# Chunked state scan feeding a gated feed-forward: the scan of chunks 2 to 5 rearranged by pairs, with B and C turned on VectorE

## The chip, the cores and the metric

One core of a Trainium2 chip runs the whole program, in one launch. The metric is the device time of one execution in microseconds: 369.13 us for the kernel before, the median of three runs (368.94 to 369.47). TensorE (PE) has two clock levels, 1.2 and 2.4 GHz; the profile gives the granted clock as a share of the higher one.

## The reference

```python
# x (4, 8, 768, 32), a (4, 8, 768), B and C (4, 8, 768, 16): batch, head, position, width
state = np.zeros((batch, H, N, D))
for c in range(S // 32):                      # 32 positions at a time
    xc, Bc, Cc, la = ...                      # la = log(clip(a, 1e-6, 1))
    cum = np.cumsum(la, axis=-1)
    M = einsum('bhin,bhjn->bhij', Cc, Bc) * tril(exp(cum_i - cum_j))
    y_intra = einsum('bhij,bhjd->bhid', M, xc)
    y_inter = einsum('bhin,bhnd->bhid', Cc, state) * exp(cum)
    y[:, :, sl] = y_intra + y_inter
    state = exp(sum(la)) * state + sum_j(Bc x xc * exp(cum_last - cum_j))
x = y as rows of 8 * 32 = 256, 3072 of them
out = (sigmoid(x @ w_gate) * (x @ w_val)) @ w_out      # 256 -> 1536 -> 256
```

How long the pieces are in which the state is carried on doesn't change the result; the kernel takes 64 positions.

## The kernel before

**Tiling.** The sequence is cut into 6 chunks (`c`) of 128 positions. A chunk of one batch entry `b` is a unit, `u = 4 c + b`; two units make a pair. The scan of a unit gives 128 rows of `x`, its two halves of 64 positions being the pieces between which a state is carried. The feed-forward pass of chunk `k` takes 512 rows at once: 12 groups `f` of 128 hidden columns, each with a gate and a value product (`pg`, `pv`, six matmuls each since operands are split into a high and a low part), then four output projections (`po`). Chunk 0 has cheaper passes with fewer parts.

**The scan of a unit** (class `Unit`, `results`). `products` (L424): TensorE turns B and C by two transposes against the identity (L431, L432) into a PSUM tile `pt`, ScalarE copies them out (L435) and writes two copies of C masked by `of_g` (L437), so that a strip of 32 partitions, which holds two heads, gives the products of each head apart. `multiply` (L486): 16 matmuls C B of a pair into `pcb` (L495). `decays`: a scan on VectorE makes the decays `ab` (L450), GpSimd multiplies B by the last of them (`bd`, L460) and C by the running products `pp` (`cd`, L472). `weigh`: VectorE multiplies the products by the decays (`m`, L509). `results`, for a pair: sums within the halves (`inside`, L526), what each half adds to the state (`keep`, L537), VectorE masks that (`chosen`, L545) and carries the state on (L572, L482), then the products of C and the state accumulate into the same PSUM columns (L581). ScalarE and VectorE take the sum out as a high and a low part of `x` (L595, L601).

**What sets the order.** Every step yields its engine, an estimated cost, what it needs and what it makes. A planner in `run` (L193) keeps a clock for each engine from these estimates and always takes the step that could start first; among those within 0.1 us the one with the earliest due time, from the call or the table `DUES` (L18). Each engine then runs its instructions in that fixed order. The scan of chunk `c` is due during the pass of chunk `c - 1`, so its pieces on TensorE stand between gate, value and projection groups. SP issues all loads and stores of that time in one queue. Three PSUM buffers serve gate, value and projection groups. The decays go through DRAM (`a_z`, `a_p`) to be spread over partitions.

Of the kernel before, what the change touches and what calls it, by code (L numbers as in the profile page):

```python
# [50 lines left out]
P0 = 18.0  # L51
# [6 lines left out]
UNIT_T = 14.9  # L58
UNIT_D = 0.0
# [12 lines left out]
def tile_ssd_then_gated_ffn(  # L72
# [26 lines left out]
    NPRE = 5  # L99
# [190 lines left out]
    def pair_of(tag, c, b, shape):  # L290

        k = tag, c, b // 2
        if k not in got:
            got[k] = ld.tile([P, 2, H, shape], F32, tag=tag, name=f"{tag}{c}_{b // 2}", bufs=2)
        return got[k]

    def load_bc(c, b, n):
        cs = slice(c * L, (c + 1) * L)
        for tag, src in (("bn", b4), ("cn", c4)):
            t = pair_of(tag, c, b, N)  # L300
            nc.sync.dma_start(
                t[:, b % 2 : b % 2 + n].rearrange("p b h n -> p (b h) n"), src[cs, b * H : (b + n) * H]
            )

# [22 lines left out]
    def load_p(c, b):  # L327
        t = ld.tile([P, L], F32, tag="pp", name=f"pp{c}_{b}", bufs=NPRE)
        src = a_p[b, :, c * L : (c + 1) * L].rearrange("h (o l) -> h o l", o=1).broadcast_to([H, N, L])
        nc.sync.dma_start(t, src)  # L330
        got["pp", c * NB + b] = t
# [80 lines left out]
    def state_of(u, name):  # L412

        return wk.tile([P, NG * D], F32, tag=f"st{u % NB}", name=f"{name}{u}", bufs=3)

    class Unit:


        def __init__(self, c, b):
            self.c, self.b, self.u = c, b, c * NB + b  # L420
            self.nm = f"{c}_{b}"
            self.more = c < NCH - 1

        def products(self):  # L424
# [9 lines left out]
            self.bct = wk.tile([P, 4, L], F32, tag="bct", name=f"bct{self.nm}", bufs=4)  # L434
# [21 lines left out]
        def decayed(self):  # L456
            c, b, u = self.c, self.b, self.u
            eng = yield step(("dve", "pool"), (0.28, 0.42), [("bc" if c else "b0", u if c else u // 2), ("scan", u), ("y", u - 4)], [("bdec", u)], port=True)
# [6 lines left out]
        def before(self):  # L465
# [5 lines left out]
            self.cd = wk.tile([P, L], F32, tag="cd", name=f"cd{self.nm}", bufs=4)  # L471
            engines[eng].tensor_tensor(out=self.cd, in0=self.bct[:, 1], in1=got["pp", u], op=ALU.mult)  # L472

        def last(self, i):
            return got["pp", self.u][:, i * L2 + L2 - 1 : (i + 1) * L2]

        def state(self):
# [3 lines left out]
            states[u] = state_of(u, "sn")  # L481
            nc.vector.scalar_tensor_tensor(  # L482
                out=states[u], in0=self.s1, scalar=self.last(1), in1=self.after, op0=ALU.mult, op1=ALU.add
            )

# [64 lines left out]
    def results(*two):  # L550
# [3 lines left out]
        c, more = two[0].c, two[0].more  # L554
# [4 lines left out]
        yield step("pe", 0.2 + 0.45 * n, needs, [("y", u) for u in us], port=96 * n if more else 80 * n)  # L559
        py = two[0].banks[:, :, 2 * L :].rearrange("p (i k) (s u l) -> p i k s u l", i=2, s=2, l=L2)  # L560
        for k, t in enumerate(two):
            within(
                t, lambda i, kt, rows: py[rows, i, kt, 0, k], lambda i, rows: py[rows, i, 0, 1, k], lambda kt: k == 0, more
# [5 lines left out]
        for k, (t, u) in enumerate(zip(two, us)):  # L569
            yield step("dve", 0.24, [("S", u - NB), ("pp", u), ("inter", u - NB)], [("first", u)], port=True)  # L570
            t.s1 = state_of(u, "sm")
# [3 lines left out]
        yield step("pe", 0.2 + 0.3 * n, [("cd", u) for u in us], [("inter", u) for u in us], port=32 * n)  # L575
# [11 lines left out]
        for i in range(2):  # L587
# [8 lines left out]
            end = {"cb": -1} if i and not more else {}  # L596
            made = [("x", c, t.b) for t in two] if i else []
            if i and not more:
                made += [(k, u) for u in us for k in ("lo", "S", "after")]
            yield step("dve", DVE_HALF, [], made, **end)  # L600
            nc.vector.tensor_tensor(out=lo, in0=y, in1=hi.bitcast(F32), op=ALU.subtract)  # L601
        if more:
            yield step("dve", 0.25, [("S", u - 2) for u in us], [(k, u) for u in us for k in ("lo", "after")], cb=-1)
            ml = wk.tile([P, n, NG * D], F32, tag="mr", name=f"mr{two[0].nm}")
            chosen(ml, py[:, 1, 0, 1], n)
            for k, t in enumerate(two):
                t.after = ml[:, k]

    class FirstUnit(Unit):
# [21 lines left out]
        def before(self):  # L631
# [3 lines left out]
            self.cd = wk.tile([P, L], F32, tag="cd", name=f"cd{self.nm}", bufs=4)  # L635
# [78 lines left out]
    def first_states(late):  # L714
# [9 lines left out]
        if late:  # L724
            for b in range(NB):
                i, k = b // 2, b % 2
                yield step("dve", 0.24, [("p0",)], [("S", b)] + ([("first", 2), ("first", 3)] if b == NB - 1 else []), port=True)
                states[b] = state_of(b, "sn")
# [107 lines left out]
    def value(k, f):  # L836
# [124 lines left out]
    a_p = dr.tile([NB, H, S], F32, name="a_p")  # L961
    a0 = const.tile([2 * NB * H, L], F32, name="a0")
# [4 lines left out]
    az, ap = (hp.tile([NB * H, S], F32, tag=f"h{10 - i}", name=f"a{i}") for i in range(2))  # L967
# [44 lines left out]

    def loads_of(c, b, n):
# [4 lines left out]
            "b": load(2, 1.6 * n, [(k, u) for k in ("tp", "bdec") for u in old], [("bc", u) for u in us], lambda: load_bc(c, b, n)),  # L1018
# [3 lines left out]
    def decays_of(c, b):  # L1022
        u = c * NB + b
        return {
            "a": load(2, 0.95, [("mult", u - NDEC), ("bdec", u - NDEC), ("a_z",)], [("a", u)], lambda: load_a(c, b)),
            "p": load(1, 0.3, [("cd", u - NPRE), ("S", u - NPRE), ("a_p",)], [("pp", u)], lambda: load_p(c, b)),
        }

    def initial():
# [3 lines left out]
        made += [("S", u) for u in range((NCH - 1) * NB, NCH * NB)]  # L1033
# [12 lines left out]
        "p": load(1, 2.3, [("p",)], [("a_p",)], save_p),  # L1046
    }
# [20 lines left out]
    def unit(due, c, b):  # L1068
        u = Unit(c, b) if c else FirstUnit(c, b)
        if c > 0:  # L1070
            if b % 2 == 0:
                for k, g in loads_of(c, b, 2).items():
                    task(due - AHEAD, f"{k}{u.nm}", g)
            for k, g in decays_of(c, b).items():
                task(due - AHEAD, f"{k}{u.nm}", g)
        else:
            task(-9.0 + b, f"spread{b}", u.spread())
        if c or b > 1:
            task(due, f"before{u.nm}", u.before())
        if c:  # L1080
            task(due, f"products{u.nm}", u.products())
        task(due, f"decays{u.nm}", u.decays())
        if c == 0 and b % 2:
# [7 lines left out]
        elif b % 2:  # L1091
            if u.u < NB * NCH - 1:
# [4 lines left out]
        if u.more and c:  # L1097
            task(due + STATE, f"state{u.nm}", u.state())

# [4 lines left out]
    for b in range(NB):  # L1104
        unit(UNIT1 + UNIT1_D * b, 1, b)
    for i in range(NW):
# [3 lines left out]
    for k in range(NCH):  # L1110
        for b in range(NB):
# [49 lines left out]
```

## Time and profile before

| | |
|---|---|
| median of 3 runs | 369.13 us |
| profiled execution | 369.12 us |
| its span | 367.3 us |
| TensorE busy | 359.9 us, 98% |
| VectorE, ScalarE, GpSimd busy | 157.1, 150.4, 152.5 us |
| granted TensorE clock | 1.00 |

The span is from the first to the last instruction of the profiled execution. fp32 matmuls leave two records each in the trace. Matmuls are pipelined: the duration of one overlaps the next, so what a piece costs is read from when the following one starts, and the chain of waits lists exactly these steps.

### The profile page before, as it was taken

What the parts mean: (1) busy time and instruction counts of PE and PEld (TensorE: products, weight loads), DVE (VectorE), ACT (ScalarE), POOL (GpSimd) and SP (SyncE); (2) the same over time, 40 slices, a digit from 0 to 9 for tenths busy, and PEclk for the clock granted to TensorE, in tenths of its full rate; (3) what the DMA queues carried; (4) which work ended last, traced back from release to release, by engine and by line L of the source; (5) the groups of instructions that cost most, each with busy time, mean ns of one, the idle gap of its engine ahead of it and who ended that gap; (6) DMA issues with size and microseconds to landing.
All of it is one profiled execution on the core that took longest, in us unless ns stands there. A gap on an engine that the chain in (4) does not pass through costs nothing.

```text
span 367.3 us, 8116 instructions
## 1 busy us (share of the span) xinstructions
PE 359.9 (98%) x3372; PEld 285.8 (78%) x3372; DVE 157.1 (43%) x279; ACT 150.4 (41%) x309; POOL 152.5 (42%) x160
## 2 busy tenths in 40 slices
PE   8999899999999999999999999999999999999996
PEld 3567478778878788788788877788877888888885
DVE  5779478774326650253551225432243510223201
ACT  2575875324573411544411454421445420343400
POOL 5435865645896400445410355520244330154410
PEclk9999999999999999999999999999999999999999
DMA  7999975545033431314031015321000000000000
GB/s 164 220 246 214 322 222 150 87 62 142 0 30 87 63 85 55 33 57 59 16 87 53 21 12 107 43 32 37 31 2 2 2 0 29 30 0 0 2 29 29
DMA packets 89270, 26.27 MB, mean 72 GB/s; under 512 B 76306, under 2 KB 82002, under 8 KB 89234
## 3 DMA queue, kind: packets, MB, share of 16 engines
q1 hardware_dynamic: 85074, 25.37, 30.1%
q10 hardware_dynamic: 4160, 0.39, 0.9%
q8 instruction: 26, 0.43, 0.5%
q14 instruction: 10, 0.08, 0.1%
HBM read 22.41 MB, written 3.34 MB: 70 GB/s over the span
## 4 chain that ended last, share of the span: by engine, by line
PE 92%; DVE 1%; ACT 1%; issue 0%
PE pv L893 25%; PE pg L893 25%; PE po L931 15%; PE po L932 7%; PE po L920 6%; PE pcb L526 2%; PE pcb L581 2%; PE pcb L495 2%; PE pv L790 1%; PE pg L790 1%; PE pcb L537 1%; PE pv L884 1%; PE pg L884 1%; PE pt L431 1%; PE po L928 1%; PE pt L432 1%
## 5 line engine op out<-in xcount | busy, mean ns | idle before, releaser
L861 POOL TENSOR_TENSOR h<-g,h 128x512 fp32r<-128x512 f32 x60 | 78.9, 1315 | 153.8 <-ACT h L859 153.3
L893 PE MATMUL pv<-xh,w 128*128 128x512 f32 x264 | 94.0, 397 | 0.0
L893 PE MATMUL pg<-xh,w 128*128 128x512 f32 x264 | 93.7, 395 | 0.0
L855 DVE TENSOR_TENSOR g<-pv,g 128x512 f32<-128x512 f32 x60 | 41.5, 692 | 97.4 <-PE pv L893 94.4
L931 PE MATMUL po<-w,h 128*128 128x512 f32 x228 | 81.9, 402 | 0.0
L859 ACT CAST h<-g 128x512 fp32r<-128x512 f32 x60 | 37.2, 621 | 79.7 <-DVE g L855 79.7
L932 PE MATMUL po<-w,h 128*128 128x256 f32 x228 | 64.0, 281 | 0.0
L893 PEld LDWEIGHTS pg<-xh,w 128*128 128x128 f32 x264 | 49.5, 188 | 11.1 <-issue 0.4
L893 PEld LDWEIGHTS pv<-xh,w 128*128 128x128 f32 x264 | 49.6, 188 | 10.7 <-issue 0.5
L893 PE MATMUL pg<-xl,w 128*128 128x512 f32 x132 | 51.5, 390 | 0.0
L893 PE MATMUL pv<-xl,w 128*128 128x512 f32 x132 | 51.5, 390 | 0.0
L931 PEld LDWEIGHTS po<-w,h 128*128 128x128 f32 x228 | 42.8, 188 | 11.0 <-issue 0.3
L834 ACT ACTIVATE g<-pg 128x512 f32<-128x512 f32 x68 | 40.8, 600 | 13.9 <-PE pg L893 13.5
L932 PEld LDWEIGHTS po<-w,h 128*128 128x128 f32 x228 | 43.1, 189 | 0.2
L949 DVE TENSOR_TENSOR o<-po,o 128x256 f32<-128x256 f32 x20 | 8.5, 425 | 53.7 <-ACT o L947 53.7
L947 ACT COPY o<-po 128x256 f32<-128x256 f32 x20 | 7.5, 373 | 54.7 <-PE po L932 54.1
L394 POOL TENSOR_TENSOR w<-wr,w 128x512 fp32r<-128x512 f32 x18 | 25.3, 1406 | 9.1 <-ACT w L392 9.1
L893 PEld LDWEIGHTS pg<-xl,w 128*128 128x128 f32 x132 | 24.8, 188 | 5.1 <-issue 0.2
L893 PEld LDWEIGHTS pv<-xl,w 128*128 128x128 f32 x132 | 24.8, 188 | 4.5
L377 POOL TENSOR_TENSOR wr<-wr 128x512 int32<-128x512 int32 x18 | 20.4, 1140 | 13.5 <-ACT wr L375 7.4
L450 DVE TENSOR_TENSOR_SCAN ab<-ab,delta 128x512 f32<-128x512 f32 x20 | 24.9, 1256 | 0.8 <-DMA ab<-a_z 0.8
L920 PE MATMUL po<-wr,h 128*128 128x256 f32 x96 | 23.4, 393 | 0.0
(105 smaller groups left out, 368.2 us busy)
## 6 DMA issues: line engine op xcount, KB each, us to landing
ab<-a_z SPq DMA_DIRECT2D x40, 128.0 KB
wr<-in_moe_w_gate_dram SPq DMA_DIRECT2D x6, 512.0 KB
wr<-in_moe_w_val_dram SPq DMA_DIRECT2D x6, 512.0 KB
wr<-in_moe_w_out_dram SPq DMA_DIRECT2D x6, 512.0 KB
out_dram<-o SPq DMA_DIRECT2D x24, 128.0 KB
xn<-in_x_dram SPq DMA_DIRECT2D x10, 256.0 KB
bn<-in_B_dram SPq DMA_DIRECT2D x10, 128.0 KB
cn<-in_C_dram SPq DMA_DIRECT2D x10, 128.0 KB
```

What stands on the lines that cost most here:

```text
L377: nc.gpsimd.tensor_tensor(out=lw.bitcast(I32), in0=hw.bitcast(I32), in1=lw.bitcast(I32), op=ALU.add)
L394: engines[eng].tensor_tensor(out=lo, in0=lw, in1=hi.bitcast(F32), op=ALU.subtract)
L450: nc.vector.tensor_tensor_scan(out=t.rearrange("p h l -> p (h l)"), data0=t.rearrange("p h l -> p (h l)"), data1=delta.rearrange("p h l -> ...
L834: nc.scalar.activation(gs[k, f], pm, AF.Sigmoid)
L855: nc.vector.tensor_tensor(out=g, in0=pm, in1=g, op=ALU.mult)
L859: copies[eng](hh, g)
L861: engines[eng].tensor_tensor(out=hl, in0=g, in1=hh.bitcast(F32), op=ALU.subtract)
L893: nc.tensor.matmul(pm, w[:, part, kt, fs], xx[:, kt], start=(i == 0), stop=(i == 3 * NK - 1))
L920: nc.tensor.matmul(acc[:, :DM], hs[k, f][:, js], whole[NF + f // 2][:, f % 2], start=start, stop=stop, skip_group_check=True,)
L931: nc.tensor.matmul(acc, hh, w.rearrange("p i m -> p (i m)"), start=start, stop=False, skip_group_check=True)
L932: nc.tensor.matmul(acc[:, :DM], hl, w[:, 0, :], start=False, stop=stop, skip_group_check=True)
L949: nc.vector.tensor_tensor(out=o, in0=acc[:, DM:], in1=o, op=ALU.add)
```

## The change

From chunk 2 on, pairs replace units (class `Pair`; chunks 0 and 1 stay as they are).

- B and C are loaded as rows of 64 numbers by eight DMAs into `tn`, 32 partitions of positions for each strip, and one VectorE instruction turns its 32 x 32 blocks (`turn`). In the result a strip of 32 partitions holds two heads of one unit, where before each strip held two heads `2q`, `2q + 1` of the unit in hand; the two units of the pair lie side by side. B is loaded as before as well (`bn`); C no more.
- The decay products are written to DRAM a second time in that order (`a_q`, four DMAs), and the states of chunk 1 are copied into it by 16 small copies of 32 partitions (`shuffled`).
- On TensorE, `block` issues without a break the products across of one pair (`across`), the products C B of the pair after next (`meet`) and the sums within of the pair between (`one_inside`, `kept`). The blocks follow one another in a chain of needs.
- Products across get PSUM columns of their own; ScalarE copies the sums within out (`inner`), VectorE adds the products across (`result`), and the low part of `x` may be taken by GpSimd.
- `az` and `ap` change their tiles, so that the value product of group 9 of chunk 0 waits for `a_z` and that of group 10 for `a_q`.

```diff
 DUES = {
-    "r": -31, "w6": -30, "w9": -25, "w11": 13, "w12": 14, "w13": 15, "w14": 16, "w15": 12.7, "w16": -2.4, "w17":
...
+    "decays3_0": 144.7, "inner5_2": 189.4, "decays5_1": 159.1, "b4_2": -39.7, "inner4_0": 101.9, "decays4_2": 139.1,
...
+    def load_t(c, b):
+        t = ld.tile([P, 2, 2 * NG, RUN * N], F32, tag="tn", name=f"tn{c}_{b // 2}", bufs=1)
+        got["tn", c, b // 2] = t
+        for q in range(NQ):
+            for k, src in enumerate((Bm, Cm)):
+                rows = src.rearrange("b h s n -> (b h) (s n)")[b * H + 4 * q : b * H + 4 * q + 4]
+                nc.sync.dma_start(
+                    t[32 * q : 32 * q + 32, k],
+                    rows[:, c * L * N : (c + 1) * L * N].rearrange("h (s x) -> s h x", x=RUN * N),
+                )
...
+    def shuffled(late):
+        for k in range(2):
+            for m in range(NQ):
+                u, q, j = NB + 2 * late + k, 2 * k + m // 2, m % 2
+                last = [("pS", 2 + late)] if k and m == NQ - 1 else []
+                eng = yield step(("act", "pool"), (0.22, 0.2), [("S", u)], last)
...
+    def meet(pcb, t):
+        t.banks = pcb
+        for j in range(2):
+            for q in range(NQ):
+                qs = slice(32 * q, 32 * q + 32)
+                for i in range(2):
+                    half = slice(i * L2, (i + 1) * L2)
+                    nc.tensor.matmul(
+                        pcb[half, q, j * L : (j + 1) * L], t.bt(j)[qs, half], t.cm(j)[qs, :, half], start=True, stop=True
+                    )
...
+    def kept(t, i, out, start=True):
+        for j in range(2):
+            for m in range(2):
+                at = 32 * (t.b % 2 * 2 + m)
+                keep_one(t, i, 2 * m + j, out[at : at + 32, j * NG * D : (j + 1) * NG * D], start and j == 0)
+
+    def across(out, state, cd):
+        for j in range(2):
+            for i in range(2):
+                for q in range(NQ):
+                    qs = slice(32 * q, 32 * q + 32)
+                    nc.tensor.matmul(
+                        out[q][j * L2 : (j + 1) * L2, i * L2 : (i + 1) * L2], state[i][qs, j],
+                        cd[qs, j, i * L2 : (i + 1) * L2], start=True, stop=True, skip_group_check=True,
+                    )
+
+    class Pair:
...
+        def turn(self):
+            p = self.p
+            yield step("dve", 1.15, [("tn", p)] + ..., [("turn", p)], port=True)
+            self.bct = wk.tile([P, 8, L], F32, tag="bct", name=f"bct{self.nm}", bufs=2)
+            nc.vector.transpose(
+                self.bct[:, :4].rearrange("p k (b r) -> p r k b", r=RUN),
+                got["tn", self.c, self.p % 2].rearrange("p k h (r n) -> p r (k h) n", n=N),
+            )
+            yield step("act", 1.02, [], [("masked", p)])
+            for g in range(NG):
+                nc.scalar.mul(
+                    self.bct[:, 4:].rearrange("p (j g) l -> p j g l", g=NG)[:, :, g], self.bct[:, 2:4], of_g[:, g : g + 1]
+                )
...
+        def inner(self):
...
+            nc.scalar.copy(self.y.rearrange("p i k u l -> p (i k) (u l)"), fixed["banks"][:, :, 2 * L : 3 * L])
+
+        def result(self):
...
+                if k:
+                    for m in range(2):
+                        nc.vector.tensor_tensor(out=y[:, m], in0=outer[m], in1=y[:, m], op=ALU.add)
+                else:
+                    more = fixed["banks"][:, :2, 3 * L :].rearrange("p m (i l) -> p m i l", i=2)
+                    nc.vector.tensor_tensor(out=y, in0=more, in1=y, op=ALU.add)
...
+                nc.scalar.copy(hi, y)
+                eng = yield step(("dve", "pool"), (DVE_HALF, 0.76), [], ..., port=True)
+                engines[eng].tensor_tensor(out=lo, in0=y, in1=hi.bitcast(F32), op=ALU.subtract)
+
+    def block(n, last, cb, now):
+        needs, makes, cost, instructions, buffers = [("block", n - 1)], [("block", n)], 0.3, 0, {}
+        if last:
+            needs += [("pfirst", last), ("pcd", last), ("added", last - 1)]
...
+        if cb:
+            needs += [("masked", cb)] + ([("mult", t.u) for t in pairs[cb - 1].two] if cb > FIRST_P else [])
...
+        if now:
+            needs += [(k, t.u) for t in pairs[now].two for k in ("mult", "bdec")]
+            needs += [("xnp", now), ("inner", now - 1), ("pafter" if now < 2 * NCH - 1 else "pfirst", now - 1)]
...
-                7: [("scan", 3)], 8: [("p",)], 9: [("a_p",)], 10: [("a_z",)],
+                7: [("scan", 3)], 8: [("p",)], 9: [("a_z",)], 10: [("a_q",)],
...
+    blocks = [(None, 4, None), (None, 5, 4)] + [(p - 1, p + 1, p) for p in range(5, 2 * NCH - 1)]
+    blocks += [(2 * NCH - 2, None, 2 * NCH - 1), (2 * NCH - 1, None, None)]
```

TensorE in the pass of chunk 1, before: the first pair of chunk 2 (`pcb_1360`), its products and its sums; `pt` is a transpose of B or C of another unit, `pg` and `pv` are gate and value groups.

```order
L893 MATMUL pg_7_1345<-xh_965,w_599 128x512
L495 MATMUL pcb_1360<-bct_0_1156 64x128 x8
L495 MATMUL pcb_1360<-bct_1_1341 64x128 x8
L431 MATMUL pt_2_1379<-eye,bn_1_1028 128x128
L432 MATMUL pt_2_1379<-eye,cn_1_1030 128x128
L893 MATMUL pv_7_1385<-xh_965,w_617 128x512
...
L893 MATMUL pv_8_1419<-xh_965,w_677 128x512
L526 MATMUL pcb_1360<-m_0_1392,xn_0_929 32x64 x16
L537 MATMUL pcb_1360<-xn_0_929,bd_0_1101 32x64 x8
L526 MATMUL pcb_1360<-m_1_1398,xn_0_929 32x64 x16
L537 MATMUL pcb_1360<-xn_0_929,bd_1_1201 32x64 x8
L893 MATMUL pg_9_1481<-xh_965,w_637 128x512
```

TensorE in the same pass, now: block 2, with the products across of chunk 2's first pair (`cd2_0`), the products of chunk 3's first (`bct3_0`) and the sums of chunk 2's second (`m2_2`, `m2_3`).

```order
L1147 MATMUL pv1_4_1432<-xh1_941,w5_1204 128x512
L715 MATMUL banks_1172<-cd2_0_1263,sq0_1018 64x64 x3
L715 MATMUL local_1268<-cd2_0_1263,sq0_1018 64x64
L715 MATMUL banks_1172<-cd2_0_1263,sm4_1355 64x64 x3
L715 MATMUL local_1268<-cd2_0_1263,sm4_1355 64x64
...
L673 MATMUL banks_1172<-bct3_0_1386 64x128 x16
L689 MATMUL banks_1172<-m2_2_1349,xn2_1_1169 32x64 x16
L689 MATMUL banks_1172<-m2_3_1359,xn2_1_1169 32x64 x16
L696 MATMUL local_1268<-xn2_1_1169,bd2_2_1165 32x64 x4
L696 MATMUL banks_1172<-xn2_1_1169,bd2_2_1165 32x64 x4
...
L1147 MATMUL pg1_5_1533<-xh1_941,w4_1149 128x512
```

Pieces that stood alone between full-size groups now stand in one run, of three different pairs, and no transpose of B or C is among them.

VectorE in the pass of chunk 1, before: value products (`g1_5` and so on) around the weighting of chunk 2's first pair (`m2_0`, `m2_1`).

```order
L855 TENSOR_TENSOR g1_5_1308<-pv1_5_1301,g1_5_1308 128x512
L855 TENSOR_TENSOR g1_6_1334<-pv1_6_1327,g1_6_1334 128x512
L509 TENSOR_TENSOR m2_0_1392<-pcb8_1360,ab2_0_810 128x512
L509 TENSOR_TENSOR m2_1_1398<-pcb8_1360,ab2_1_748 128x512
L855 TENSOR_TENSOR g1_7_1377<-pv1_7_1385,g1_7_1377 128x512
L855 TENSOR_TENSOR g1_8_1426<-pv1_8_1419,g1_8_1426 128x512
L450 SCALAR_TENSOR_TENSOR ab3_2_1400<-ab3_2_1400,delta_100 128x512
```

VectorE at the start of the same pass, now: between block 0 and block 2.

```order
L682 TENSOR_TENSOR m2_0_1206<-banks_1172,ab2_0_800 128x512
L682 TENSOR_TENSOR m2_1_1213<-banks_1172,ab2_1_897 128x512
L740 STREAM_TRANSPOSE bct2_2_1230<-tn2_1_1109 128x4x128
L1109 TENSOR_TENSOR g1_0_1225<-pv1_0_1217,g1_0_1225 128x512
L1109 TENSOR_TENSOR g1_1_1265<-pv1_1_1254,g1_1_1265 128x512
L682 TENSOR_TENSOR m2_2_1349<-banks_1172,ab2_2_946 128x512
L582 TENSOR_TENSOR ml2_0_1353<-local_1268,mask_102 128x128
L682 TENSOR_TENSOR m2_3_1359<-banks_1172,ab2_3_1020 128x512
L659 SCALAR_TENSOR_TENSOR sm4_1355<-sq0_1018,pp2_0_1190,ml2_0_1353 128x64
L740 STREAM_TRANSPOSE bct3_0_1386<-tn3_0_1243 128x4x128
L1109 TENSOR_TENSOR g1_2_1368<-pv1_2_1361,g1_2_1368 128x512
```

The weightings of chunk 2 have moved to the start of the pass, and two of the eight new transposes stand among them and the first value products.

## Rows read from the trace of the kernel before

**Rows 1.** Page, busy time of each engine and granted clock in 40 slices.

```profile
PE 359.9 (98%) x3372; PEld 285.8 (78%) x3372; DVE 157.1 (43%) x279; ACT 150.4 (41%) x309; POOL 152.5 (42%) x160
...
PEclk9999999999999999999999999999999999999999
```

**Rows 2.** Waits of TensorE, longest in total: us in total, times, longest us.

```profile
PE pt L431 <- ACT bct L437: 1.0, 1, 1.0
...
PE pcb L526 <- DVE m L509: 0.2, 1, 0.2
```

**Rows 3.** Table by stage: from:to, length, PE, PEld, DVE, ACT, POOL busy, clock, DMA.

```profile
88.57:144.88 56.31, 56.31 (x568) 46.10 (x567) 24.46 (x41) 23.63 (x48) 30.21 (x29) 1.00 0.26 53
144.88:201.49 56.61, 56.61 (x569) 46.23 (x569) 21.75 (x40) 20.67 (x44) 18.94 (x20) 1.00 0.27 52
201.49:258.43 56.94, 56.94 (x571) 46.43 (x571) 19.36 (x38) 21.68 (x47) 19.96 (x21) 1.00 0.23 42
258.43:314.50 56.07, 56.07 (x536) 45.62 (x535) 16.73 (x30) 19.92 (x41) 16.80 (x15) 1.00 0.04 11
314.50:367.30 52.80, 49.54 (x241) 41.52 (x239) 10.85 (x18) 16.50 (x29) 15.48 (x12) 1.00 0.05 15
```

**Rows 4.** Chain that ended last, in order of time: start us, us, what.

```profile
80.09 3.82 PE po L920 x16
...
114.37 0.38 PE pcb L526 x32
114.75 0.20 PE pcb L537 x9
...
115.28 0.21 PE pcb L537 x12
115.49 1.59 PE pg L893 x6
...
265.26 0.11 PE pt L431
...
266.87 1.36 PE pg L893 x6
268.23 0.62 PE pcb L495 x32
268.85 1.59 PE pv L893 x6
...
288.54 0.62 PE pcb L581 x32
```

**Rows 5.** TensorE in order of time, chunk 0: start us, us, instruction, records.

```profile
20.42 0.86 PE L526 MATMUL pcb<-m,xn 64*32 64x64 f32 x64
21.20 0.69 PE L691 MATMUL pcb<-cd,m 32*64 32x64 f32 x32
```

**Rows 6.** Groups on VectorE by form: count, busy us, mean ns, idle before.

```profile
L450 DVE TENSOR_TENSOR_SCAN ab<-ab,delta 128x512 f32<-128x512 f32 x20 | 24.9, 1256 | 0.8 <-DMA ab<-a_z 0.8
L509 DVE TENSOR_TENSOR m<-pcb,ab 128x512 f32<-128x512 f32 x24 | 15.7, 686 | 5.8 <-PE pcb L495 5.6
...
L572 DVE SCALAR_TENSOR_TENSOR sm<-sn,pp,ml 128x64 f32<-128x64 f32 x20 | 7.9, 426 | 0.4
...
L545 DVE TENSOR_TENSOR ml<-pcb,mask 128x128 f32<-128x128 f32 x10 | 2.9, 290 | 15.9 <-PE pcb L537 15.9
...
L996 DVE TENSOR_TENSOR_SCAN a<-a,a 32x768 f32<-32x768 f32 x1 | 2.9, 2864 | 0.0
```

**Rows 7.** Group on ScalarE, masked copies of chunk 0.

```profile
L659 ACT ACTIVATE bct<-pt,of_g 128x256 f32<-128x256 f32 x4 | 1.7, 479 | 0.0
```

**Rows 8.** SP in order of time: start us, us, DMA issues.

```profile
49.24 5.54 SPq L322 DMA_DIRECT2D ab<-a_z  x8
...
57.40 1.13 SPq L322 DMA_DIRECT2D ab<-a_z  x2
```

**Rows 9.** VectorE in order of time, scans of chunk 1: start us, us, idle before.

```profile
61.32 1.23 DVE L450 TENSOR_TENSOR_SCAN ab<-ab,delta 128x512 f32<-128x512 f32 x1 [0.82 <-DMA ab<-a_z]
...
67.69 2.06 DVE L450 TENSOR_TENSOR_SCAN ab<-ab,delta 128x512 f32<-128x512 f32 x1
```

More of the change, by code (lines that the diff above doesn't have):

```diff
@@ L57 @@
 FFN1 = 82.0
-UNIT_T = 14.9
-UNIT_D = 0.0
+EARLY = (15.0, 35.0)
 AHEAD = 46.7
@@ L292, in pair_of @@
         k = tag, c, b // 2
+        if tag == "cn" and k not in got:
+            both = ld.tile([P, 2, 2, H, N], F32, tag="tn", name=f"cn{c}", bufs=1)
+            for late in range(2):
+                got[tag, c, late] = both[:, late]
         if k not in got:
@@ L484, in state, with cd_of @@
             )
+    def cd_of(u):
+        k = "cd", u // 2
+        if k not in got:
+            got[k] = wk.tile([P, 2, L], F32, tag="cd", name=f"cd{u // 2}", bufs=2)
+        return got[k][:, u % 2]
     def multiply(pcb, at, *us):
@@ L553, in results @@
         n = len(two)
-        c, more = two[0].c, two[0].more
+        c = two[0].c
         for t, u in zip(two, us):
@@ L595, in results @@
             nc.scalar.copy(hi, y)
-            end = {"cb": -1} if i and not more else {}
             made = [("x", c, t.b) for t in two] if i else []
-            if i and not more:
-                made += [(k, u) for u in us for k in ("lo", "S", "after")]
-            yield step("dve", DVE_HALF, [], made, **end)
+            yield step("dve", DVE_HALF, [], made)
             nc.vector.tensor_tensor(out=lo, in0=y, in1=hi.bitcast(F32), op=ALU.subtract)
[L602 to L607, printed above, removed]
+        yield step("dve", 0.25, [("S", u - 2) for u in us], [(k, u) for u in us for k in ("lo", "after")], cb=-1)
@@ new lines, in results @@
+        ml = wk.tile([P, n, NG * D], F32, tag="mr", name=f"mr{two[0].nm}")
+        chosen(ml, py[:, 1, 0, 1], n)
+        for k, t in enumerate(two):
+            t.after = ml[:, k]
+    def shuffled(late):
[4 more added lines that the diff above has]
+                eng = yield step(("act", "pool"), (0.22, 0.2), [("S", u)], last)
+                if 2 + late not in states2:
+                    states2[2 + late] = state_of(late, "sq")
+                (nc.scalar.copy if eng == "act" else nc.gpsimd.tensor_copy)(
+                    states2[2 + late][32 * q : 32 * q + 32, j], states[u][32 * m : 32 * m + 32]
+                )
@@ new lines, in spread_out, with one_inside @@
+    def spread_out(t, pcb):
+        k = t.b % 2
+        t.m = wk.tile([P, H, L2], F32, tag="m", name=f"m{t.nm}", bufs=4)
+        by = "p (q h) l -> p q (h l)"
+        nc.vector.tensor_tensor(
+            out=t.m.rearrange(by, q=2), in0=pcb[:, 2 * k : 2 * k + 2, : 2 * L], in1=t.dec.rearrange(by, q=2), op=ALU.mult
+        )
+    def one_inside(t, i, kt, r, out, start):
+        half, h = slice(i * L2, (i + 1) * L2), NQ * kt + r
+        nc.tensor.matmul(
+            out, got["xn", t.c, t.b // 2][half, t.b % 2, h], t.m[half, h], start=start, stop=True, skip_group_check=True
+        )
@@ L966, in tile_ssd_then_gated_ffn @@
     )
-    az, ap = (hp.tile([NB * H, S], F32, tag=f"h{10 - i}", name=f"a{i}") for i in range(2))
+    az, ap = (hp.tile([NB * H, S], F32, tag=f"h{9 + i}", name=f"a{i}") for i in range(2))
     load_first("cn", c4, 0, N, nc.scalar)
@@ L1032, in initial @@
         made = [(k, u) for k in keys for u in range(-6, 0)]
-        made += [("S", u) for u in range((NCH - 1) * NB, NCH * NB)]
+        made += [(k, p) for k in ("plo", "pafter", "inner", "added") for p in range(2, FIRST_P)] + [("block", -1)]
         made += [("used", i) for i in (-2, -1)] + [(k, u) for k in ("cd", "inter") for u in range(2)]
@@ L1096, in unit @@
             pair.append(u)
-        if u.more and c:
+        if c:
             task(due + STATE, f"state{u.nm}", u.state())
+            if b % 2:
+                task(due + STATE, f"shuffle{b // 2}", shuffled(b // 2))
     task(-20.0, "products0", first_products())
@@ L1105, in tile_ssd_then_gated_ffn @@
         unit(UNIT1 + UNIT1_D * b, 1, b)
+    starts = [P0, FFN1] + [FFN1 + (2 * NF * GV_T / 2 + NB * PROJ_T) * k for k in range(1, NCH)]
+    for c in range(2, NCH):
+        for b in range(NB):
+            unit(starts[c - 2] + EARLY[b // 2] if c > 2 or b > 1 else starts[1] - EARLY[0], c, b)
+    blocks = [(None, 4, None), (None, 5, 4)] + [(p - 1, p + 1, p) for p in range(5, 2 * NCH - 1)]
+    blocks += [(2 * NCH - 2, None, 2 * NCH - 1), (2 * NCH - 1, None, None)]
+    for i, (last, cb, now) in enumerate(blocks):
+        if i < 4:
+            due = starts[1] + (2.0, 10.0, 25.0, 40.0)[i]
+        else:
+            due = starts[2 + (i - 4) // 2] + (14.0, 38.0)[(i - 4) % 2]
+        task(due, f"block{i}", block(i, last, cb, now))
     for i in range(NW):
@@ L1110, in tile_ssd_then_gated_ffn @@
     for k in range(NCH):
-        for b in range(NB):
-            if k + 1 < NCH and k:
-                unit(t + UNIT_T + UNIT_D * b, k + 1, b)
         for i, f in [(i, f) for i in range(2) for f in range(NF) if halved(k, f)]:
```

221 lines of the change are left out of this document (190 added, 31 removed), and 26 rows, old and new, of the table DUES.

## The prediction

> **What bounds the kernel now.** I read the busy shares first. TensorE is busy for 98% of the span, every other engine for 43% or less, its granted clock full in every slice [rows 1]. So the question is whether those 98% are work or waits, which the list of TensorE's waits answers: behind the warm-up the longest is 1.0 us, and the only one on a piece of the scan is 0.2 us [rows 2]. TensorE is the bound as a sequence: from 44 us on, the run lasts as long as its matmuls take one after the other, and a microsecond less on another engine is worth nothing.
>
> The table by stage shows how much of that sequence is the scan [rows 3]. The four stretches from 88.57 to 314.50 us are the feed-forward passes of chunks 1 to 4, each with the scan of the next chunk strewn in. The last, from 314.50 us, is the pass of chunk 5 alone, with 49.54 us of TensorE. All passes have the same matmuls, so the scan costs the surplus: 56.31 - 49.54 = 6.77, then 7.07, 7.40 and 6.53, together 27.77 us. Of the 16 pairs of transposes of chunks 2 to 5 these stretches hold 15; the other adds 0.22. In all 27.99 us for eight pairs of units, 3.5 us a pair, is what the change works on.
>
> The chain of waits prices the pieces, by when the next group of matmuls comes [rows 4]. An undisturbed gate or value group of six takes 1.36 us. A transpose takes 0.11, two 0.22. The products of a pair (L495) take 0.62, and the group behind them 1.59 in place of 1.36, so 0.23 more. The sums within a pair (L526 and L537) take 115.49 - 114.37 = 1.12, again with 0.23 behind them. The products across (L581) take 0.62. Much of a pair's cost is coming and going: three pieces at 0.23 each, and the transposes.
>
> **The change part by part.** On TensorE it removes the 32 transposes of chunks 2 to 5. The matmuls of the scan stay, shape for shape: for each pair 16 products, 32 sums within, 16 state sums (8 in the last chunk), 16 products across. They stand in ten blocks where there were 24 pieces: one with products alone, one with products and sums, six with all three, one with products across and sums, one with products across alone. By the rows that is
>
> - products across 8 x 0.62 = 4.96, products 8 x 0.62 = 4.96,
> - sums 8 x 1.12 = 8.96, less 0.20 for the two pairs of the last chunk (L537 holds 0.20 + 0.21 of the 1.12; of the half of that I take half),
> - coming and going 10 x 0.23 = 2.30,
>
> together 20.98, which is 27.99 - 20.98 = 7.01 us less.
>
> Two things about the blocks no row prices. Within seven or eight of them the shape goes from 32 rows x 64 columns of the array to 64 x 32. The nearest place is in chunk 0, where 64 records of L526 run straight into L691, the other way about: L691 begins 0.78 us after them [rows 5], and 32 such records last 0.38 in the chain [rows 4]. So the step costs between 0.78 - 2 x 0.38 = 0.02 and, if the second 32 ran free beside the first, 0.40. The state sums of a unit now go to two strips of the array's columns instead of four; if they ran at half the rate, the 0.41 of L537 would come on top once more in each block. Against both stands what a block may save: the 0.62 of a piece alone holds its own fill and drain, which three in a row may share, up to 0.23 less at each seam. I take 0.05 for each shape step, 0.40 together, because 0.02 comes from records of one kind and 0.40 from an assumption, and set the strips against the shared drains, keeping both ends for the range.
>
> The Trainium skill speaks to this (TensorEngine Tiling (Array Packing), section Key Properties): changing the tiling mode, not just the tile, drains TensorE. The rows agree at the border to full-size matmuls, 0.23 each time. By the rule the inner step costs a border of its own, and the sum would be 8 x 0.18 = 1.4 us worse than mine; that lies within rival A.
>
> VectorE gets eight transposes of 512 elements a lane. No row shows one. From below stands the elementwise product of 512 at 0.69, near it the scan of 512 at 1.26, and the dearest row by element is the scan of 768 in 2.86, 3.73 ns each, which makes 1.91 of 512 [rows 6]. I take 1.26, since like the scan it is no plain elementwise form. VectorE also adds three sums a pair to the results and may leave the low halves of x to GpSimd. All that lies beside TensorE's groups and costs only where a block stands waiting for it, so I looked in the order for the shortest covers.
>
> Block 1 comes four groups behind block 0, 4 x 1.36 = 5.44 us. In between stand two weightings at 0.69 and the transpose on VectorE, then on ScalarE two masked copies of 256 elements at 0.48 [rows 7] and perhaps a cast of 512, taken as two of these: 1.38 + 1.26 + 0.96 + 0.96 = 4.6. It fits by 0.9.
>
> That transpose waits for its own load, eight issues on SP that begin only when the transpose before has freed the one buffer. An issue takes 0.56 (two in 1.13), and a load issued from 57.40 to 58.53 [rows 8] was waited for until 61.32 [rows 9], 2.8 us: 8 x 0.56 + 2.8 = 7.3 us. The cover runs from behind the sums of chunk 1's last pair over four projection steps of 1.91 (two in 3.82 [rows 4]), one piece across and block 0 at 0.85 each and the two weightings: 7.64 + 1.70 + 1.38 = 10.7, less 2.0 until the first transpose is done. It fits by 1.4.
>
> The products across of chunk 1's last pair have that first transpose ahead: 0.29 + 0.43 + 1.26 + 0.43 = 2.4 us against two steps, 3.82. Block 7 comes 5.44 us behind block 6; ahead of it VectorE has a mask at 0.29 twice, two weightings, two state updates at 0.43 and three sums of 128 or 256 elements, at most 0.49 each (midway between the rows of 128 and 512): 4.3. It fits by 1.1. Behind each such instruction the value groups' products queue on VectorE; with three PSUM buffers one may come a group late before TensorE feels it.
>
> Moved on SP: four writes of a second copy of the decay products go ahead of the loads of chunk 1's decay products, and the value product of group 10 now waits for them. They are issued from 54.8 [rows 8] to 54.8 + 4 x 0.56 = 57.0 and by the 2.8 us are there at 59.8. That product now has a second scan and a weighting ahead of it and comes no earlier than 57.4 + 2 x 1.26 + 0.69 = 60.6. No wait; 2 us later, VectorE would stand 1.2 and TensorE less.
>
> For all waits together I allow 0.15 us, near the 0.2 that the scan waits now.
>
> The profiled execution took 369.12 us, 367.3 the span and 1.8 around it; the median of the three runs is 369.13, so nothing is to be corrected. 369.12 - 7.01 + 0.40 + 0.15 = **362.7 us**, 1.7% faster.
>
> **The rivals.**
>
> A, the blocks are dearer than the pieces. Shape step 0.40 in eight and strips 0.41 in seven (the last chunk's count half): 6.1 at the worst, two thirds of it 4.1: 366.3 us. For it: L537 takes 0.41 for 21 records where L526 takes 0.38 for 32, slow already. Against it: shapes and counts are those of before.
>
> B, the blocks are cheaper. In 14 seams two pieces share 0.23, 3.2 us: 359.0 us.
>
> C, slower than before: the transpose on VectorE is so slow that TensorE waits for it. Its three tight places leave it 3.82 - 1.15 = 2.7, 5.44 - 3.30 = 2.1 and, ahead of block 2 (six groups, 8.16 us, less 4.9 for two weightings and three value products at 0.69, two masks and two state updates), 3.3 us. A transpose of length T makes TensorE wait (T - 2.7) + (T - 2.1) + (T - 3.3); that eats the gain of 6.4 at T = 4.8 us, and at 6 the time is 372.6 us. Against it: 4.8 is four times the scan. For it: the output has a stride of four elements, and VectorE's rows stretch beside other work, a scan from 1.23 to 2.06 [rows 9].
>
> The Trainium skill has a rule for that stride (SBUF — State Buffer, Specifications (TRN2)): an SBUF line is 16 bytes, and access that goes to a new line each time pays. Four fp32 are such a line; the page has no price. No row here writes so; if it doubled the 0.69, the transpose would take 1.4 and nothing above would change.
>
> D, no change: A at its worst, 368.3, with a transpose of 3 us, 0.3 + 0.9 more: 369.5.
>
> **How the numbers follow.** The forecast has 0.55, with 360.9 to 364.9 as its own range; A 0.16, B 0.09, C 0.12, D 0.08. A difference under 0.2%, 0.74 us, can't be told from none here. Faster is forecast, A and B, 0.80; within it D, 0.08; slower C, 0.12. The range leaves out C, most of D and the far end of B: 359.4 to 368.4.
>
> **What would show it.** TensorE's transposes end with chunk 1, and the pass of chunk 4 takes 49.6 us, since all blocks lie before it. A full block moves the next group by 2.6 us (A: over 3.0; B: under 2.2). TensorE's waits after 44 us stay under 1 us in all. VectorE's transpose takes 0.7 to 1.9. I am wrong if in more than one place a block's first matmul waits over half a microsecond for VectorE, ScalarE, GpSimd or a load, or if the full blocks cost the 3.5 us of the pieces that they replace.

## The result and the profile after

The changed kernel takes 362.24 us (median of 4 runs, 361.98 to 362.64) against 369.03 us (368.49 to 369.47) beside it: a ratio of 0.9818, 95% interval 0.9801 to 0.9835. It is 6.8 us faster, where 6.4 us were forecast.

First the page's line of busy times, which answers to [rows 1]:

```profile
PE 352.4 (98%) x3340; PEld 283.5 (79%) x3340; DVE 165.4 (46%) x295; ACT 151.4 (42%) x298; POOL 166.6 (46%) x171
```

TensorE has 32 instructions fewer, the transposes (3372 before), and 7.5 us less to do; its share stays at 98%. VectorE has 8 us more, GpSimd 14, and neither matters for the end, as the rest shows.

The table by stage, with the columns of [rows 3]. The boundaries are the first matmul of block 0, of block 4, and the first gate of chunks 3, 4 and 5:

```profile
88.35:145.83 57.48, 57.48 (x728) 47.58 (x730) 36.45 (x60) 27.99 (x57) 35.44 (x35) 1.00 0.48 105
145.83:201.21 55.38, 54.81 (x561) 45.96 (x562) 22.99 (x44) 20.02 (x38) 22.09 (x23) 1.00 0.28 58
201.21:258.01 56.80, 56.80 (x689) 47.07 (x689) 19.51 (x44) 20.68 (x39) 23.37 (x24) 1.00 0.07 18
258.01:307.61 49.60, 49.60 (x242) 41.76 (x241) 10.00 (x16) 16.11 (x28) 15.46 (x12) 1.00 0.03 11
307.61:360.20 52.59, 49.55 (x241) 41.55 (x239) 10.85 (x18) 16.48 (x29) 15.46 (x12) 1.00 0.05 16
```

The pass of chunk 4 is a pure pass now. The four stretches together are 307.61 - 88.35 = 219.26 us; less four pure passes of 49.54 that leaves 21.10 us for the scan of chunks 2 to 5, where before it was 27.99 [rows 3]. The difference, 6.89 us, is nearly all of the 7.14 by which the two profiled executions differ (369.12 and 361.98). Three of the four stretches have no idle TensorE at all; the second has 0.57 us.

One full block (block 2, all three pieces) in the chain that ended last, start and duration in us:

```profile
104.88 0.21 PE banks L715 x3
...
105.31 0.65 PE banks L673 x25
105.96 0.72 PE banks L689 x49
...
107.13 1.59 PE pg L1147 x6
```

Products across 105.31 - 104.88 = 0.43, products of the next pair 0.65, sums (L689 and L696) 107.13 - 105.96 = 1.17, and the group behind them 0.23 over its 1.36. The next group moves by 2.25 + 0.23 = 2.48 us; the pieces that this replaces moved it by 3.5 [rows 4].

TensorE's waits from 44 us on, columns of [rows 2]:

```profile
PE po L1185 <- issue: 0.6, 1, 0.6
```

It is the only one, it is new, and it has no releaser. The kernel before has none from 44 us on: the wait of 0.2 on a piece of the scan [rows 2] lies at 12 us, in chunk 0, and is still there. The new one stands 0.9 us behind block 5:

```profile
192.59 0.57 issue
193.16 0.51 PE po L1185
```

The matmul behind it took 0.51 where its like take 0.24, so the stop costs 0.84 us. In the DMA queues of the 0.5 us from 190.5 stands one packet on the queue for instructions (packets, MB, share of 16 engines; 26 of them are 0.43 MB in the whole run, so 16 KB each):

```profile
q8 instruction: 1, 0.02, 15.7%
```

By its count this queue is TensorE's: 26 packets stand against 3340 matmul records and 3340 of weight loads, 257 for each packet. In the passes without scan, packets fall at 262.5, 291.0, 316.0 and 342.5 us, and TensorE has 255, 265 and 243 such records between them.

Last, the new transpose on VectorE, columns of [rows 6]:

```profile
L740 DVE STREAM_TRANSPOSE bct<-tn 128x512 f32<-128x512 f32 x8 | 8.8, 1104 | 1.9 <-DMA tn<-in_C_dram 0.8 <-POOL cd L757 0.6 <-issue 0.5
```

1.10 us each.

### The profile page after: what moved, and what is told of

Its sections match the earlier page's. It is cut to its first block, busy times and chain, and to the rows that moved or that the text cites. A ratio compares the mean times of both kernels' runs of the same rounds, so it can differ in the third digit from the quotient of the medians.

```text
span 360.2 us, 8117 instructions
## 1 busy us (share of the span) xinstructions
PE 352.4 (98%) x3340; PEld 283.5 (79%) x3340; DVE 165.4 (46%) x295; ACT 151.4 (42%) x298; POOL 166.6 (46%) x171
## 4 chain that ended last, share of the span: by engine, by line
PE 92%; DVE 1%; ACT 1%; issue 0%
PE pg L1147 25%; PE pv L1147 25%; PE po L1185 15%; PE po L1186 8%; PE po L1174 6%; PE banks L689 2%; PE pv L1044 1%; PE banks L673 1%; PE pg L1044 1%; PE pv L1138 1%; PE pg L1138 1%; PE banks L715 1%; PE po L1182 1%; PE local L696 0%; PE po L1193 0%
## 5 line engine op out<-in xcount | busy, mean ns | idle before, releaser
L1115 POOL TENSOR_TENSOR h<-g,h 128x512 fp32r<-128x512 f32 x60 | 79.7, 1329 | 112.0 <-ACT h L1113 112.0
L1147 PE MATMUL pv<-xh,w 128*128 128x512 f32 x264 | 92.5, 391 | 0.0
L480 DVE TENSOR_TENSOR_SCAN ab<-ab,delta 128x512 f32<-128x512 f32 x20 | 26.9, 1354 | 7.1 <-DMA ab<-a_z 7.1
L398 POOL TENSOR_TENSOR wr<-wr 128x512 int32<-128x512 int32 x18 | 21.9, 1224 | 12.7 <-ACT wr L396 6.6
```

What stands on the lines that cost most here:

```text
L398: nc.gpsimd.tensor_tensor(out=lw.bitcast(I32), in0=hw.bitcast(I32), in1=lw.bitcast(I32), op=ALU.add)
L480: nc.vector.tensor_tensor_scan(out=t.rearrange("p h l -> p (h l)"), data0=t.rearrange("p h l -> p (h l)"), data1=delta.rearrange("p h l -> ...
L1115: engines[eng].tensor_tensor(out=hl, in0=g, in1=hh.bitcast(F32), op=ALU.subtract)
L1147: nc.tensor.matmul(pm, w[:, part, kt, fs], xx[:, kt], start=(i == 0), stop=(i == 3 * NK - 1))
```

## The experiments

The theory: the run is TensorE's sequence, and the gain is what left it, 3.5 us of transposes and 14 borders (goings from small to full-size matmuls) at 0.23. Rivals: the gain came from elsewhere (other engines, cheaper pieces), or VectorE's transposes cost something that hides in the sum. The medians of the groups of runs differ by a few tenths, and the start of block 0 moves from 87.5 to 89.1 us between runs. So beside the times I compare the stretch from block 0's first matmul to the last step of the chain; in the changed kernel it is 357.17 - 88.35 = 268.82 us.

**Transposes put back on TensorE.** In each of 16 steps:

```
+ for i in range(2):
+     nc.tensor.transpose(t[:, 2 * L + i * L : 3 * L + i * L], eye, eye)
```

> The changed kernel with 32 transposes of 128 by 128 added on TensorE, two in each of sixteen steps behind blocks 1 to 8; nothing reads them. VectorE still does the transposes that are used. Theory: of the gain of 6.8 us the transposes are 32 x 0.11 = 3.5 us, so the time rises by 3.5 us, to 365.7 (0.9 more or less where a stop for instructions comes or goes). Rival: transposes of full size hide in the stream, and the gain is the borders or the other engines' relief: under 0.7 us more, below 363.

Measured 366.96 us (ratio to before 0.9948, 0.9933 to 0.9963), 4.7 over the changed kernel. The chain shows a pair in the stream and one right behind a block:

```profile
107.31 0.37 PE local L869 x2
...
124.73 0.22 PE local L869 x2
```

Sixteen pairs at 0.22 are 3.5 us. The stretch is 4.36 us longer, and the chain has two places for the rest:

```profile
116.27 1.65 PE pg L1155 x6
...
193.95 0.88 issue
```

The chain comes to 116.27 through a product on VectorE: TensorE begins that group some 0.3 us late, and it takes 1.65 in place of 1.36. The stop now falls inside block 5, which takes 3.43 us (191.82 to 195.25) in place of 2.25; it costs 1.18 where it was 0.84. With these 0.9 us the sum closes. The transposes do not hide: the first half of the gain is shown.

**The pieces apart.** Three steps in place of one, and in the planner:

```
+ if eng == "pe" and name.startswith("block") and last_pe[0].startswith("block"):
+     continue
```

> The changed kernel with each block taken apart into its pieces (products across; products; sums), in the same order, with at least one full-size group of TensorE between two of them. Same matmuls, same work on all other engines. Theory: fourteen borders come back at 0.23 each, 3.2 us, and the seven or eight pieces across cost 0.62 alone where they take 0.43 in a block, 1.4 us: 4.6 us more, less 0.85 if the stop for instructions behind block 5 goes: 366.0 to 366.8 us. Rival 1: only the borders count: 365.4. Rival 2: joining the pieces brought nothing, the transposes all: 362.2, within 0.5.

Measured 366.52 us (0.9940, 0.9927 to 0.9952). Block 6 in its chain:

```profile
206.96 0.21 PE banks L719 x3
...
207.41 1.58 PE pg L1140 x6
208.99 0.62 PE banks L677 x32
209.61 1.59 PE pv L1140 x6
211.20 0.72 PE banks L693 x49
...
212.38 0.66 PE pg L1140 x2
```

Each piece has its border again, 1.58 or 1.59 in place of 1.36: 14 more at 0.23 are 3.2 us. But the time fits for another reason than I gave. The piece across takes 207.41 - 206.96 = 0.45 alone, not 0.62, and the sums 1.18: pieces share nothing by standing in a row. In place of my 1.4 us stand two new waits for VectorE:

```profile
PE pg L1140 <- DVE g L1102: 1.2, 1, 1.2
...
PE banks L693 <- DVE m L686: 0.7, 1, 0.7
```

3.2 + 1.9 - 0.84 (the stop behind block 5 is gone) is 4.3 of the 4.6 us by which the stretch grew. Borders shown; the shared drain refuted.

**Two inner steps.** The lines of the products across moved behind the sums, within the block.

> The changed kernel with the pieces of a block in the order products, sums, products across: in the six full blocks the tile shape changes twice within a block in place of once; the order of the program is the same. Theory: the inner step is worth at most 0.05, a full block goes from 2.26 to at most 2.31, the time stays within 0.3 of 362.2 us. Rival (each change of the tiling mode drains TensorE as at the borders, 0.23): 2.49 and six times 0.23 is 1.4 us more, 363.6 us.

Measured 362.07 us (0.9810, 0.9796 to 0.9824). Block 2:

```profile
105.62 0.62 PE banks L673 x32
106.24 0.72 PE banks L689 x49
...
107.42 0.21 PE banks L715 x3
...
107.86 1.58 PE pg L1147 x6
```

107.86 - 105.62 = 2.24, with two steps of shape, against 2.25 with one. A step within the block costs nothing that can be seen.

**Why the piece across is cheaper.** The kernel before, with the order of the 16 matmuls of a piece (32 records) changed by chunk:

```
+ if c == 2:
+     every = [(k, i, q) for k in range(n) for i in range(2) for q in (0, 2, 1, 3)]
+ if c == 3:
+     every = [(k, i, q) for half in range(2) for k ... for q in (half, half + 2)]
+ if c == 5:
+     every = [(k, i, q) for i in range(2) for q in range(NQ) for k in range(n)]
...
+ start=c == 4
```

> The kernel before, with the products across of a pair (32 matmuls, 0.62 us until the next group begins, where the changed kernel's take 0.45 alone) issued in another form in each chunk: chunk 1 as it is; chunk 2 the row groups in the order 0, 2, 1, 3, so that neighbours share a half of the columns; chunk 3 all of the left half of the columns first, then all of the right; chunk 4 as it is but starting the accumulation anew, which leaves out of the result what was summed before; chunk 5 the two units in turn, so that neighbours share a tile. Theory: the old form keeps to four of the array's eight tiles (each row group always meets the same half of the columns), and a matmul waits for the one before it on its tile; no order changes that: 0.62, within 0.04, in chunks 2 and 4, and as much or more in 3 and 5. Rival 1: the order of the halves counts: chunk 2 or 3 falls towards 0.45. Rival 2: adding onto what is there costs: chunk 4 falls towards 0.45.

One run, 371.03 us beside 369.43. The time says little of the pieces, since at 42 us, ahead of all of them, the granted clock (third column from the end) fell:

```profile
44.00:46.00 2.00, 2.00 (x6) 1.19 (x5) 1.00 (x2) 0.76 (x2) 2.00 (x2) 0.50 0.97 344
```

It was 0.68 from 42 to 44 us, behind waits of 1.11 and 0.61 us; in the kernel before the same two are 0.99 and 0.61, and the clock stays at 1.00. The stretch of 3.23 us (42.03 to 45.26) takes 4.87 here, 1.6 us more. At the pieces themselves the clock is full. The chain, one piece of each of chunks 1 to 5:

```profile
71.55 0.62 PE pcb L588 x32
...
121.27 0.62 PE pcb L588 x32
...
176.59 0.91 PE pcb L588 x30
177.50 1.58 PE pg L900 x6
...
229.48 0.62 PE pcb L588 x32
...
290.39 0.69 PE pcb L588 x30
```

Both rivals fail: with neighbours on one half of the columns (chunk 2), or starting a sum anew (chunk 4), it stays at 0.62. Units in turn (chunk 5) take 0.69. By the loops, the old form keeps to four tiles of the array (32 rows by 64 columns each): a row group, that is 32 of the rows, always meets the same half of the columns, 0.62. One half first and then the other (chunk 3) leaves two tiles at a time: 0.91. In the changed kernel a row group serves both halves of the columns, eight tiles: 0.45. It too has one half first, but in its trace the second half's products with the pair's first state (`sq`) and the first half's with its second (`sm`) start among each other:

```profile
104.97 0.22 PE L715 MATMUL banks<-cd,sm 32*64 32x64 f32 x1
104.97 0.22 PE L715 MATMUL banks<-cd,sq 32*64 32x64 f32 x1
```

The Trainium skill says that tiles work independently and in parallel (TensorEngine Tiling (Array Packing), section Key Properties); the three numbers agree. One rival is left for the step from 0.62 to 0.45, and no run tests it: in the changed kernel each row group writes a 512-column part of the PSUM tile, or a PSUM tile, of its own, where before two row groups wrote into one part.

**The strips of the state sums.** Loops turned:

```
- for one in t.two:
-     for i in range(2 if t.more else 1):
-         kept(one, i, fixed["local"][i])
+ for j in range(2):
+     for m in range(2):
+         for one in t.two:
+             for i in range(2 if t.more else 1):
...
+                 keep_one(one, i, 2 * m + j, ...)
```

> The changed kernel with the state sums of a pair in another order: both units and both halves of the rows in turn, so that neighbouring matmuls go to four strips of columns and two of rows, in place of two strips and one. Same matmuls. Theory (the strips term that I had set to nothing): 32 state sums take 0.45 us in a block where 64 sums within take 0.72, that is 0.36 for 32; in turn they take 0.36, seven and a half blocks times 0.09 is 0.7 us less, 361.5 us. Rival: the matmuls are limited one by one, not by the strip: 0.45 stays, 362.2 us.

Measured 362.12 us (0.9811, 0.9795 to 0.9827), by the time no difference. In its chain block 2 runs from 105.10 to 107.28, 2.18 in place of 2.25, and so do the other four like it; the sixth, in the last chunk with half the state sums, goes from 2.13 to 2.09. So this order is worth 0.07 to 0.08 a block. The time hides it, because the stop behind block 5 grew from 0.57 to 0.96.

**The stop.** Block 5 ahead of the rest of its projection:

```
+ "block5": 166.5,
```

> The changed kernel with block 5 placed ten projection matmul pairs earlier, all else the same work. In the trace of the changed kernel TensorE stands 0.57 us at 192.59, 0.9 us behind block 5, with no releaser, and its next matmul takes 0.51 in place of 0.24: 0.85 us in all; a 16 KB packet on the instruction queue falls into 190 to 191. Theory: the block's 320 instructions use up one such packet's worth in under 2 us, so that two fetches of instructions come closer than one takes; 80 instructions earlier the second falls 4 us or more behind the block and the stop goes: 0.85 us less, 361.4 us, and no wait without a releaser behind block 5. Rival: the stop comes from the load of x that is issued behind the block or from the block itself: it moves along, 362.2 us.

Measured 361.82 us (0.9810, 0.9797 to 0.9822). No wait without a releaser is left, and the stretch is 356.88 - 88.89 = 267.99, 0.83 shorter, as expected. The medians show 0.4 of it; in the profiled execution block 0 began 0.5 later. In six programs with the stop, TensorE goes on 2.4 to 2.9 us behind a 16 KB packet on the instruction queue: packet at 190.5, 191.1, 191.9, 190.9, 190.6 and 200.6, going on at 193.16, 193.51, 194.82, 193.36, 193.05 and 203.03 (the changed kernel, strips in turn, transposes back, two inner steps, transpose twice, four times). But for the first and fifth, 0.1 us apart, the later the packet, the later TensorE. The rival is out, for the block and the load of x behind it are still there. That TensorE waits for its own instructions fits all of this and is argued, not shown: no run changes their loading alone. Why the packet comes at another time in programs with the same TensorE instructions stays open.

**VectorE's transpose twice and four times.** `for _ in range(2)` and `range(4)` around it.

> The changed kernel with each of VectorE's eight transposes done twice, one behind the other into the same tile; the order of the program is the same. A transpose takes 1.10 us, so T goes to 2.2. Theory: VectorE lies beside TensorE's groups, with covers of 2.7, 2.1 and 3.3 us at the three tightest places: TensorE waits 0.1 us more, the time stays within 0.3 of 362.2 us. Rival: the eight transposes lie on the path and the time rises by up to 8 x 1.1, to between 364 and 371 us.

> The changed kernel with each of VectorE's eight transposes done four times into the same tile; the order of the program is the same. T goes to 4.4 us. By the covers of rival C TensorE waits (4.4 - 2.7) + (4.4 - 2.1) + (4.4 - 3.3) = 5.1 us: 367.3 us. Rival 1: the covers are wider than worked out: under 364 us. Rival 2: each of the eight places waits or value groups come late behind it as well: over 370 us.

Twice: 362.15 us (0.9810, 0.9793 to 0.9828), no difference, with 8.9 us more on VectorE. Four times: 372.79 us (1.0101, 1.0080 to 1.0122), 10.6 more, twice what I worked out; its profiled execution took 371.82, 9.8 more. TensorE's waits in its trace that the changed kernel's does not have:

```profile
PE pg L1148 <- DVE g L1110: 3.2, 3, 2.2
PE pv L1148 <- DVE g L1110: 1.7, 1, 1.7
...
PE banks L673 <- ACT bct L747: 1.1, 1, 1.1
...
PE pcb L618 <- DVE sm L609: 0.8, 1, 0.8
...
PE pv L1148 <- DVE o L1204: 0.3, 1, 0.3
```

7.1 us. Only 1.1 is a block waiting for its transpose through the masked copies, and 0.8 the piece across of chunk 1 waiting for a state update. 4.9 are gate and value groups that want a PSUM buffer, which VectorE's product of a value group (L1110) has not freed. For 2.7 of these it queues right behind a transpose of 4.5 us. The longest, 2.2, comes another way: ahead of that product VectorE itself stood for a late load of decays.

```profile
157.29 1.23 DVE L480 TENSOR_TENSOR_SCAN ab<-ab,delta 128x512 f32<-128x512 f32 x1 [2.66 <-DMA ab<-a_z]
...
160.19 0.68 DVE L1110 TENSOR_TENSOR g<-pv,g 128x512 f32<-128x512 f32 x1
```

The load was issued at 153.16, and the chain goes from there back through SP's queue to a transpose that ended at 150.24. A group behind a wait also takes longer, 1.66 in place of 1.36:

```profile
107.20 1.66 PE pv L1148 x6
```

And part of the rest is the clock. TensorE in order of time (start, us, instruction, idle before) and the stretch from 161 us with its granted clock:

```profile
160.93 0.50 PE L1148 MATMUL pg<-xh,w 128*128 128x512 f32 x1 [2.21 <-DVE g L1110]
...
161.50 1.04 PE L1148 MATMUL pg<-xh,w 128*128 128x512 f32 x2
...
162.76 0.63 PE L1148 MATMUL pg<-xh,w 128*128 128x512 f32 x1
163.19 0.63 PE L1148 MATMUL pv<-xh,w 128*128 128x512 f32 x1
...
164.90 0.42 PE L1148 MATMUL pv<-xl,w 128*128 128x512 f32 x1
```

```profile
161.00:164.00 3.00, 3.00 (x8) 2.40 (x9) 2.93 (x4) 0.54 (x1) 1.29 (x1) 0.58 0.89 162
```

Behind a wait of 2.21 us the granted clock goes to 0.58 of full in these 3 us, that is mostly the lower of its two levels (1.2 of 2.4 GHz). A matmul starts every 0.43 us in place of 0.23, until 164.90: eight of them (161.50 to 164.90) lose 3.4 - 8 x 0.23 = 1.6 us. Rival 2 of the expectation holds, in its second half: value groups come late.

**All in turn.** The strips, block 5 earlier, and two loops more:

```
  def across:  - for j ... for i ... for q     + for i ... for q ... for j
  def meet:    - for j ... for q ... for i     + for j ... for i ... for q
```

> The changed kernel with block 5 placed earlier, the state sums in turn over the strips, the products across with the two halves of the columns in turn, and the products of a pair with the four row groups in turn. Same matmuls. From the first runs: block 5 earlier takes out the stop of 0.85 us, the sums in turn take 0.08 off a full block (2.26 to 2.18) and 0.04 off the short ones. Theory (neighbouring matmuls on different tiles of the array overlap better): the products across go from 0.45 towards 0.38, the products from 0.65 towards 0.60, so a full block comes to 2.06 to 2.18 and the time to 360.2 to 361.0 us. Rival: these two are limited by the issue of their 64 instructions: a block stays at 2.18 and the time comes to 361.0 us or more.

Measured 360.76 us (360.07 to 361.03), ratio to before 0.9772, 0.9758 to 0.9787: the fastest of all, its interval apart from the changed kernel's. Block 4:

```profile
145.12 0.23 PE banks L715 x6
...
145.53 0.61 PE banks L673 x28
146.15 0.72 PE banks L689 x49
...
147.25 1.60 PE pg L1150 x6
```

Across 0.41, products 0.61, sums 1.10, together 2.13. The stretch is 355.15 - 87.54 = 267.61, 1.2 shorter; blocks (0.9 over the ten) and stop (0.84) alone would make 1.7. Two groups of that run took 0.22 and 0.25 longer with no reason in the trace, which closes the sum.

## Why the prediction was right

The time, the mechanism and the signs came as forecast: no transposes behind chunk 1, the pure pass at 49.60, a full block at 2.48 (between 2.2 and 3.0), a wait of 0.6 us. That the sum came within 0.4 us of the medians is partly luck: by the table its terms are 2.0 us too dear in some places and 1.3 too cheap in others, and most of that cancels. Term by term, before to after:

| term | predicted | measured | from |
|---|---|---|---|
| transposes | -3.52 | -3.52 | 32 x 0.11; 0.22 a pair in the stream put back |
| borders, 24 to 10 | -3.22 | -3.3 | seven of 0.23 behind a gate or value group, three of 0.19 in a projection |
| products across | 0 | -1.5 | for 0.62 six times 0.43, twice 0.45 |
| sums | -0.20 | +0.2 | for 1.12 six times 1.17, then 1.06 and 1.04 |
| products | 0 | +0.2 | 0.65 for 0.62 in a block |
| shape steps | +0.40 | 0 | 2.24 with two, 2.25 with one |
| waits | +0.15 | +0.84 | the stop behind block 5 |
| together | -6.4 | -7.1 | the table by stage has -6.89; 0.2 is not placed |

- **Bound by the sequence: shown.** Eight transposes of 2.2 us on VectorE instead of 1.1 change nothing; 32 of 0.11 on TensorE cost their full length. It holds as long as the covers do: at 4.4 us TensorE waits.
- **Products across at 0.62: the step that failed most.** I wrote that the matmuls of the scan stay, shape for shape. Their shapes do, but not the tiles that they meet, nor the place of their sums in PSUM. The row priced the old pattern.
- **Strips set to nothing against shared drains: right only in sum.** A pair's sums take 1.17 or 1.18 where they took 1.12, in a block or alone (1.18), so two strips instead of four cost at most 0.06 a pair, inside my bounds of 0 to 0.41. The 0.08 is what another order would give back. Shared drains do not show.
- **Inner steps at 0.05: too much.** By the rule of the Trainium skill that a change of the tiling mode drains TensorE (TensorEngine Tiling (Array Packing), section Key Properties) each would have cost 0.23. Here a cost shows at the border to full-size matmuls alone, and not between two modes of small tiles.
- **Waits of 0.15: mis-sized.** The 0.2 that I leaned on lies at 12 us, in chunk 0. The places that I checked held, none of their covers ran out. The stop is none of these; I had priced a block's 320 records (160 of matmuls, 160 of weight loads) by time and not by number.
- **VectorE's transpose: 1.10 for 1.26**, between the product of 512 at 0.69 and the scan. On the 16-byte lines of the Trainium skill (SBUF — State Buffer, section Specifications (TRN2)) no run tells anything, since none writes in another stride.
- **Rivals.** A and B are out by the block's 2.48. C's mechanism is real, and the point from which it decides lies lower than the 4.8 us that I gave: at 4.4 the kernel is already slower than before. Of its three places block 2 did not wait, and the other two waited 0.8 and 1.1 us where C gives 1.7 and 2.3. I had counted what a block waits for, and not the value groups behind the transpose on VectorE's queue, though the text named them, nor the loads that a late transpose holds up.

## What to carry to other kernels

When one engine is the bound as a sequence, price a change by what leaves and enters that sequence, borders between tile shapes included, and check covers for every instruction that queues behind a new one, not only for the one that needs its result. A price for small matmuls holds for the pattern of tiles that it was read from: count how many tiles a piece uses before carrying it over. Behind many tiny instructions in one place look for a wait without a releaser, and try another place for them.

## What was not expected of the hardware

- 16 matmuls (32 records) of 32 rows by 64 columns, each until the next instructions start: 0.91 us with two tiles at a time, 0.62 with four, 0.45 with eight (four, then the other four), 0.41 with eight in turn. For the last two the sums' places in PSUM differ too.
- Going between 32 x 64 and 64 x 32 tiles costs nothing measurable (2.24 and 2.25 us), going to full-size matmuls 0.19 to 0.23.
- Behind a wait of 2.2 us TensorE's granted clock was at its lower level for some 3.4 us, at a cost of 1.6 us. Behind two waits of 1.11 and 0.61 us it fell as well, at the same cost, in one run; behind 0.99 and 0.61 at the same place of the kernel before it stayed full.
- TensorE stopped 0.3 to 1.0 us at or behind a block of 160 records of small matmuls in 2.3 us, and went on 2.4 to 2.9 us behind a packet of 16 KB on the queue whose packets keep step with its instructions.
